# Long convolution and SiLU block on one core: token tiles of the second part 512 columns wide

## Chip, cores and metric

The kernel runs on 1 core of one Trainium2 chip. The metric is device time in microseconds (us). Three runs of the kernel before took 1626.51, 1628.32 and 1631.16 us; the median, 1628.32 us, is the number to beat.

## What is computed

Two parts follow one another. The first is a gated long convolution over 2 batches of 12480 tokens with 128 channels, by a transform of length 2 x 12480; the second is a two-layer block with SiLU between its weights, of 128 x 2048 and 2048 x 128:

```python
h_filt = (np.maximum(pos_emb @ w1, 0.0) @ w2) * np.exp(-0.01 * pos)[:, None]
u = x * v
y = np.fft.irfft(np.fft.rfft(u, n=L, axis=1) * np.fft.rfft(h_filt, n=L, axis=0)[None], n=L, axis=1)[:, :S]
attn = (x * y).reshape(B * S, D)
h = attn @ w_in
out = (h / (1.0 + np.exp(-h))) @ w_out
```

All is fp32. The second part takes each product as three fp32r matmuls: a value a is kept as a high part (a rounded to fp32r) and a low part (a minus the high part), and high x high, low x high and high x low are summed in PSUM.

## The kernel before

**The transform.** 12480 tokens are padded to 2 halves (i = 0, 1) of R = 98 rows by C = 64 columns. A first stage works along R (`stage_a`, L217, matmuls into tile ap), then for each of 49 pairs of frequencies a second stage goes forward (`pair_u`, tile up), multiplies by the filter and goes back (`pair_w`, tile wp; both at L419), and stores to DRAM (wd, L474). The last inverse stage is `attn_tile` (L611): for a token tile of up to five of the 64 columns it makes the blocks of 98 or 97 tokens in a PSUM bank yp, multiplies by x (L622, tile att) and splits the product into ah and al (L623, L624). Its inputs are fetched by `load_tile` (L594 from wd, L599 from x) into one buffer each.

**Token tiles.** `token_tiles` gives 52 tiles: for each batch and half twelve of five columns and one of four. Their widths are 490 (12 x), 392, 486 (12 x), 388, and the same again for the second batch, 24984 token columns in all.

**The second part** is one loop over steps (n, f), token tile n and one of NF = 16 slices f of the hidden dimension, 832 steps. A step issues three matmuls for the hidden slice (L813, L814, L815, into hq), ScalarE's SiLU (L820), the high part (L822 on VectorE, or L824 on ScalarE for some f), the low part (L825 on VectorE), and then, three steps late (`lag=3`), the three matmuls of an older slice into the output bank op (L841, L842, L843). After f = 15 the output is copied (L846) and stored. `attn_tile(n + 1)` is issued at f = 8 and `load_tile(n + 2)` at f = 9, so that ah and al of the next tile are ready before f = 0.

**What runs beside it.** The first batch's convolution is done before the loop starts, as are 7 of the 32 groups of the second batch's first stage. The rest of the second batch's convolution is a generator, `batch1_steps`, of 666 small side steps. The loop takes from it at each step in proportion, so that it has ended after `n_side` = 384 steps: two tiles before the last tile of the first batch has been used. All engines run in program order. PE gets its order from this loop, SP (the queue of loads) too: behind a load that waits for its buffer, all later loads wait. In the shared part the SiLU writes back into hq (three PSUM banks); after it, into a tile g in SBUF.

```python
steps = [(n, f) for n in range(len(tiles)) for f in range(NF)]
if f == 8 and n + 1 < len(tiles):
    attn[n + 1] = attn_tile(n + 1, *ahead.pop(n + 1), pmy, ("yp", 1))
if f == 9 and n + 2 < len(tiles):
    ahead[n + 2] = load_tile(n + 2)
while done < total and done * n_side < (s + 1) * total:
    done += next(side, total)
```

Of the kernel before, what the change touches and what calls it, by code (L numbers as in the profile page):

```python
# [10 lines left out]
F32 = mybir.dt.float32  # L11
F32R = mybir.dt.float32r
U32 = mybir.dt.uint32
AF = mybir.ActivationFunctionType
ALU = mybir.AluOpType
# [17 lines left out]
NF = DFF // 128  # L33
# [15 lines left out]
def tile_widths(i, n):  # L49

    if i == 0:
        return [98] * n
    w = [97] * n
    if n % 2:
        w[-1] = 98
    return w


def tile_offsets():
    offs, o = [], 0  # L60
    for b, i, t2, n in token_tiles():
        offs.append(o)
        o += sum(tile_widths(i, n))
    return offs, o


P = dict(
# [22 lines left out]
def kernel(  # L90
# [16 lines left out]
    nc = tc.nc  # L107
    ctx.enter_context(tc.manual_schedule())

    def pool(name, **kw):  # L110
        kw.setdefault("bufs", 1)
        return tc.alloc_tile_pool(name=name, reuse_waits="tile", **kw)
# [116 lines left out]
    def slot(o, n=512):  # L229

        return slots.rearrange("p k n -> p (k n)")[:, o : o + n]
# [128 lines left out]
    for t in P["seq"]:  # L360
# [9 lines left out]
        elif t == "p":  # L370
            g = len(pts)
            pts.append(wprep.tile([128, NP, R], F32, name=f"pt{g}", tag="pt", bufs=P["pb"]))
            for o in range(0, NP, 4) if g == 0 else [0]:
                n = 4 if g == 0 else NP
# [154 lines left out]
    pp = pool("pp2", space=PSUM)  # L529
# [6 lines left out]
    for it in range(-1, NQ):  # L536
# [7 lines left out]
        if 0 <= q < NQ:  # L544
            up = pair_u(0, q, pp, [(fbs[q][:, :, 0], X[:, 2 * q : 2 * q + 2])], nb)
            _, uw = times_i(0, q, rp, up, nb)
# [19 lines left out]
        if 0 <= q < NQ:  # L566
            hab = habs.pop(q)
            _, at = pair_p(0, q, rp, up, hab, 0, "at", nb, nc.vector)
            _, bt = pair_p(0, q, rp, uw, hab, 1, "bt", nb, nc.gpsimd)
# [15 lines left out]
    php.release()  # L585
    psa = pool("psa3", space=PSUM)
    tiles = token_tiles()
    offs, _ = tile_offsets()

    def load_tile(n):  # L590
        b, i, t2, m = tiles[n]
        w = sum(tile_widths(i, m))
        wt = slot(4096, 2 * 5 * D)[0:R].rearrange("p (c n) -> p c n", c=2)
        nc.sync.dma_start(  # L594
            out=wt[:, :, 0 : m * D],
            in_=wd[b][:, i].rearrange("k (c t) d -> k c (t d)", c=2)[:, :, t2 * D : (t2 + m) * D],
        )
        xs = slot(4096 + 2 * 5 * D, 490)
        nc.sync.dma_start(out=xs[:, 0:w], in_=xt[:, offs[n] : offs[n] + w])  # L599
        return wt, xs  # L600

    def attn_tile(n, wt, xs, psp, tag):
        b, i, t2, m = tiles[n]
        ws = tile_widths(i, m)
        w = sum(ws)
        yp = psp.tile([128, 512], F32, name=f"yp{n}", tag=tag[0], bufs=tag[1])
        o = 0
        for t in range(m):
            for c in range(2):
                for h in range(0, D, 64):  # L610
                    nc.tensor.matmul(  # L611
                        yp[h : h + 64, o : o + ws[t]],
                        wt[:, c, t * D + h : t * D + h + 64],
                        fai_sb[:, c, 0 : ws[t]],
                        start=(c == 0),
                        stop=(c == 1),
                    )
            o += ws[t]
        at = mt.tile([128, 490], F32, name=f"att{n}", tag="att", bufs=1)
        ah = mt.tile([128, 512], F32R, name=f"ah{n}", tag="ah", bufs=2)  # L620
        al = mt.tile([128, 512], F32R, name=f"al{n}", tag="al", bufs=2)
        nc.vector.tensor_tensor(out=at[:, 0:w], in0=yp[:, 0:w], in1=xs[:, 0:w], op=ALU.mult)  # L622
        nc.scalar.copy(out=ah[:, 0:w], in_=at[:, 0:w])  # L623
        nc.vector.tensor_tensor(out=al[:, 0:w], in0=at[:, 0:w], in1=ah[:, 0:w].bitcast(F32), op=ALU.subtract)  # L624
        return ah, al

    ahead, attn = {}, {}
    n_a = n_t = n_h = n_l = 0
    n_r = 4
    for t in P["seq3"]:  # L630
        if t == "x":
            uv.load()
        elif t in "md":
            uv.mul(nc.vector if t == "d" else nc.gpsimd)
        elif t in "Aa":
            stage_a_group(1, n_a, psa, uss.pop(n_a), 2, t == "A")
            n_a += 1
        elif t == "s":
            pair_s(*prods[NQ - 1])
        elif t == "v":  # L640
            pair_v(prods[NQ - 1][0], nc.vector)
        elif t == "u":
            last_w(NQ - 2)
        elif t == "U":
            last_w(NQ - 1)
            rp.release()
            rpa.release()
            mw = pool("mw")
            wo_split[:] = (mw.tile([128, NF * D], F32R, name=f"wo{k}") for k in "hl")
            mt = pool("mt")  # L650
        elif t == "S":
            nc.scalar.activation(out=warm_sb, in_=w2_sb[0:1, 0:1], func=AF.Silu)
        elif t == "L":
            ahead[n_t] = load_tile(n_t)
            n_t += 1
        elif t == "r":
            load_raw(n_r, spare[:, (n_r - 4) // 2 * 2, 256 * (n_r % 2) : 256 * (n_r % 2) + 256], wod)
            n_r += 1
        elif t == "h":
            split_hi(n_h, wo_split)  # L660
            n_h += 1
        elif t == "l":
            split_lo(n_l, wo_split)
            n_l += 1
        elif t == "Y":
            attn[0] = attn_tile(0, *ahead.pop(0), pp, ("up", 2))
    NA = n_a
    woh, wol = wo_split
    wih, wil = wi_split
# [5 lines left out]
    moe = pool("moe")  # L675
    fr = pool("fr")
    pmy = pool("pmy", space=PSUM)
# [4 lines left out]
    class Carved:  # L682


        at = dict(hab=(0,), at=(1024,), bt=(1792,), uw=(2560,), ws=(3072,), fb=(3584, 5868))
# [108 lines left out]

    pools = [psa]
    side = batch1_steps()
    n_side = (len([t for t in tiles if t[0] == 0]) - 2) * NF
    total = 2 * P['ya'] * (D // 4 - NA) + P['pd'] * NQ + max(P['off'].values()) - min(P['off'].values()) + 1
    done = 0
    steps = [(n, f) for n in range(len(tiles)) for f in range(NF)]  # L800
    LAG = P['lag']
    if P.get("cut2"):
        steps = steps[:P['cut2']]
    gs = {}
    op = {}
    for s in range(len(steps) + LAG):
        if s < len(steps):
            n, f = steps[s]
            w = sum(tile_widths(*tiles[n][1::2]))
            ah, al = attn[n]  # L810
            hp = pm.tile([128, 512], F32, name=f"hq{s}", tag="hq", bufs=3)
            fs = slice(f * 128, (f + 1) * 128)
            nc.tensor.matmul(hp[:, 0:w], wih[:, fs], ah[:, 0:w], start=True, stop=False)  # L813
            nc.tensor.matmul(hp[:, 0:w], wih[:, fs], al[:, 0:w], start=False, stop=False)  # L814
            nc.tensor.matmul(hp[:, 0:w], wil[:, fs], ah[:, 0:w], start=False, stop=True)  # L815
            beside = done < total
            g = hp if beside else moe.tile([128, 490], F32, name=f"g{s}", tag="g", bufs=2)
            gh = moe.tile([128, 512], F32R, name=f"gh{s}", tag="gh", bufs=P['lag'] + 1)
            gl = moe.tile([128, 512], F32R, name=f"gl{s}", tag="gl", bufs=P['lag'] + 1)
            nc.scalar.activation(out=g[:, 0:w], in_=hp[:, 0:w], func=AF.Silu)  # L820
            if f % P['fp'] if beside else f % P['fg']:
                nc.vector.tensor_copy(gh[:, 0:w], g[:, 0:w])  # L822
            else:
                nc.scalar.copy(out=gh[:, 0:w], in_=g[:, 0:w])  # L824
            nc.vector.tensor_tensor(out=gl[:, 0:w], in0=g[:, 0:w], in1=gh[:, 0:w].bitcast(F32), op=ALU.subtract)  # L825
            gs[s] = gh, gl
            if f == 8 and n + 1 < len(tiles):
                attn[n + 1] = attn_tile(n + 1, *ahead.pop(n + 1), pmy, ("yp", 1))
            if f == 9 and n + 2 < len(tiles):
                ahead[n + 2] = load_tile(n + 2)  # L830
            while done < total and done * n_side < (s + 1) * total:
                done += next(side, total)
        if s >= LAG:
            n, f = steps[s - LAG]
            w = sum(tile_widths(*tiles[n][1::2]))
            if f == 0:
                op[n] = pm.tile([128, 512], F32, name=f"op{n}", tag="op", bufs=2)
            o = op[n]
            fs = slice(f * 128, (f + 1) * 128)
            gh, gl = gs.pop(s - LAG)  # L840
            nc.tensor.matmul(o[:, 0:w], woh[:, fs], gh[:, 0:w], start=(f == 0), stop=False)  # L841
            nc.tensor.matmul(o[:, 0:w], woh[:, fs], gl[:, 0:w], start=False, stop=False)  # L842
            nc.tensor.matmul(o[:, 0:w], wol[:, fs], gh[:, 0:w], start=False, stop=(f == NF - 1))  # L843
            if f == NF - 1:
                ot = moe.tile([128, 490], F32, name=f"ot{n}", tag="ot", bufs=2)
                nc.scalar.copy(out=ot[:, 0:w], in_=o[:, 0:w])  # L846
                nc.scalar.dma_start(out=out[:, offs[n] : offs[n] + w], in_=ot[:, 0:w])
                del op[n], attn[n]
    if not P.get("cut2"):
        for _ in side:  # L850
# [85 lines left out]
```

## Time and profile before

| what | value |
|---|---|
| median of the runs | 1628.32 us |
| profiled execution, span from first to last instruction | 1624.7 us |
| PE busy | 1591.1 us, 98% of the span |
| VectorE (DVE) busy | 1285.6 us, 79% |
| ScalarE (ACT) busy | 1108.2 us, 68% |
| GpSimd (POOL) busy | 575.4 us, 35% |

The page gives the span of the profiled execution; no other time of that execution is recorded. It lies 3.6 us below the median of the runs. The second part's loop begins at about 329 us, the side steps end at about 988 us, and from there to the end only the second part and `attn_tile` run. PE's matmuls are pipelined: a matmul's recorded duration covers filling and draining, so the time that one more matmul costs is read from the distance between two starts.

### The profile page before, as it was taken

How to read it: one execution, taken by the hardware profiler on the slowest of the kernel's cores; microseconds unless marked ns; L12 is line 12 of the kernel's file. 1: busy time of each engine (PE TensorE's matmuls, PEld its weight loads, DVE VectorE, ACT ScalarE, POOL GpSimd, SP SyncE). 2: the span in 40 equal slices, each digit the busy share in tenths (PEclk: the TensorE clock that was granted, in tenths of full speed). 3: DMA queues.
4: the chain of work that ended last, by engine and by line, in shares of the span. 5: the costliest groups of instructions: out<-in, count | busy, mean ns of one | idle time of the engine just before them, and what ended most of it. 6: DMA issues, size and time to landing. Idle time of an engine off the chain costs nothing.

```text
span 1624.7 us, 27176 instructions
## 1 busy us (share of the span) xinstructions
PE 1591.1 (98%) x9376; PEld 1369.7 (84%) x9376; DVE 1285.6 (79%) x2182; ACT 1108.2 (68%) x2151; POOL 575.4 (35%) x564
## 2 busy tenths in 40 slices
PE   7899999899999999999999999999999999999999
PEld 6787777688888888988888888888888898888888
DVE  5979899765688889888888887777777777777776
ACT  5598898767777777777777775555555555555555
POOL 5627778632156656666666650000000000000000
PEclk9899999889999999999999999999999999999999
DMA  9838999854255554555554541111111111111110
GB/s 264 235 100 229 237 262 259 236 137 121 77 132 138 132 145 128 153 134 148 135 137 133 135 109 53 43 50 49 33 47 48 47 43 38 44 50 47 35 41 18
DMA packets 130001, 186.99 MB, mean 115 GB/s; under 512 B 11346, under 2 KB 79608, under 8 KB 129864
## 3 DMA queue, kind: packets, MB, share of 16 engines
q1 hardware_dynamic: 89480, 147.58, 33.2%
q10 hardware_dynamic: 40384, 37.67, 8.3%
q8 instruction: 75, 1.23, 0.3%
q14 instruction: 62, 0.51, 0.1%
HBM read 125.36 MB, written 53.42 MB: 110 GB/s over the span
## 4 chain that ended last, share of the span: by engine, by line
PE 79%; DMA 1%; issue 0%; SPq 0%; POOL 0%; ACT 0%; DVE 0%; POOLq 0%
PE op L841 12%; PE op L843 11%; PE op L842 11%; PE hq L814 11%; PE hq L813 11%; PE hq L815 11%; PE yp L611 6%; PE wp L419 2%; PE up L419 2%; PE ap L217 2%; DMA slots<-in_v_dram 1%; DMA slots<-wd 0%; POOL slots L245 0%; SPq L240 0%; DVE att L622 0%
## 5 line engine op out<-in xcount | busy, mean ns | idle before, releaser
L820 ACT ACTIVATE g<-hq 128x486 f32<-128x486 f32 (+3 forms) x448 | 255.6, 570 | 224.2 <-PE hq L815 214.3
L825 DVE TENSOR_TENSOR gl<-g,gh 128x486 fp32r<-128x486 f32 (+3 forms) x448 | 294.4, 657 | 94.7 <-PE hq L815 59.4
L841 PE MATMUL op<-gh,woh 128*128 128x490 f32 (+3 forms) x832 | 323.4, 389 | 0.0
L814 PE MATMUL hq<-al,wih 128*128 128x490 f32 (+3 forms) x832 | 315.9, 380 | 0.0
L813 PE MATMUL hq<-ah,wih 128*128 128x490 f32 (+3 forms) x832 | 315.8, 380 | 0.0
L843 PE MATMUL op<-gh,wol 128*128 128x490 f32 (+3 forms) x832 | 315.4, 379 | 0.0
L815 PE MATMUL hq<-ah,wil 128*128 128x490 f32 (+3 forms) x832 | 315.4, 379 | 0.0
L842 PE MATMUL op<-gl,woh 128*128 128x490 f32 (+3 forms) x832 | 315.1, 379 | 0.0
L820 ACT ACTIVATE hq<-hq 128x490 f32<-128x490 f32 (+2 forms) x384 | 214.1, 559 | 93.8 <-PE hq L815 65.6
L825 DVE TENSOR_TENSOR gl<-hq,gh 128x490 fp32r<-128x490 f32 (+2 forms) x384 | 251.7, 662 | 32.6 <-ACT gh L824 22.1
L822 DVE CAST gh<-hq 128x490 fp32r<-128x490 f32 (+2 forms) x288 | 188.9, 656 | 50.0 <-ACT hq L820 48.4
L822 DVE CAST gh<-g 128x486 fp32r<-128x486 f32 (+3 forms) x336 | 137.7, 410 | 56.9 <-ACT g L820 54.9
L813 PEld LDWEIGHTS hq<-ah,wih 128*128 128x128 f32 x832 | 156.7, 188 | 25.6 <-DVE gl L825 0.8
L814 PEld LDWEIGHTS hq<-al,wih 128*128 128x128 f32 x832 | 156.6, 188 | 24.9
L841 PEld LDWEIGHTS op<-gh,woh 128*128 128x128 f32 x832 | 156.5, 188 | 24.9
L815 PEld LDWEIGHTS hq<-ah,wil 128*128 128x128 f32 x832 | 156.7, 188 | 24.6
L843 PEld LDWEIGHTS op<-gh,wol 128*128 128x128 f32 x832 | 156.3, 188 | 25.0
L842 PEld LDWEIGHTS op<-gl,woh 128*128 128x128 f32 x832 | 156.6, 188 | 19.7 <-DVE gl L825 0.3
L223 ACT COPY X<-ap 64x392 f32<-64x392 f32 x208 | 99.8, 480 | 34.4 <-PE ap L217 32.2
L611 PEld LDWEIGHTS yp<-fai_sb,slots 98*64 98x64 f32 x2048 | 89.3, 138 | 17.9 <-issue 16.7
L611 PE MATMUL yp<-fai_sb,slots 98*64 98x98 f32 (+1 forms) x2048 | 99.4, 252 | 0.3 <-DMA slots<-wd 0.3
L623 ACT CAST ah<-att 128x490 fp32r<-128x490 f32 (+3 forms) x52 | 30.9, 594 | 90.5 <-DVE att L622 90.5
(1068 smaller groups left out, 2546.7 us busy)
## 6 DMA issues: line engine op xcount, KB each, us to landing
slots<-hs SPq DMA_DIRECT2D x98, 256.0 KB
slots<-wd SPq DMA_DIRECT2D x48, 490.0 KB
hs<-hab SPq DMA_DIRECT2D x49, 256.0 KB
wd<-ws SPq DMA_DIRECT2D x49, 256.0 KB
slots<-in_fb_dram SPq DMA_DIRECT2D x49, 256.0 KB
wd<-slots ACTq DMA_DIRECT2D x49, 256.0 KB
fb<-in_fb_dram ACTq DMA_DIRECT2D x45, 256.0 KB
xs<-in_x_dram SPq DMA_DIRECT2D x32, 196.0 KB
```

Source lines behind the costliest of these rows:

```text
L223: nc.scalar.copy(out=o, in_=src[:, k0:k1])
L419: nc.tensor.matmul(out[:, k].rearrange("p i d -> p (i d)"), f[:, k], a[:, k], start=(i == 0), stop=(i == len(passes) - 1),)
L611: nc.tensor.matmul(yp[h : h + 64, o : o + ws[t]], wt[:, c, t * D + h : t * D + h + 64], fai_sb[:, c, 0 : ws[t]], start=(c == 0), stop=(c = ...
L813: nc.tensor.matmul(hp[:, 0:w], wih[:, fs], ah[:, 0:w], start=True, stop=False)
L814: nc.tensor.matmul(hp[:, 0:w], wih[:, fs], al[:, 0:w], start=False, stop=False)
L815: nc.tensor.matmul(hp[:, 0:w], wil[:, fs], ah[:, 0:w], start=False, stop=True)
L820: nc.scalar.activation(out=g[:, 0:w], in_=hp[:, 0:w], func=AF.Silu)
L822: nc.vector.tensor_copy(gh[:, 0:w], g[:, 0:w])
L825: nc.vector.tensor_tensor(out=gl[:, 0:w], in0=g[:, 0:w], in1=gh[:, 0:w].bitcast(F32), op=ALU.subtract)
L841: nc.tensor.matmul(o[:, 0:w], woh[:, fs], gh[:, 0:w], start=(f == 0), stop=False)
L842: nc.tensor.matmul(o[:, 0:w], woh[:, fs], gl[:, 0:w], start=False, stop=False)
L843: nc.tensor.matmul(o[:, 0:w], wol[:, fs], gh[:, 0:w], start=False, stop=(f == NF - 1))
```

## The change

The second part no longer walks over the 52 token tiles. `moe_tiles` cuts the 24984 token columns into 49 spans: a first one of 408 and 48 of 512. The inverse transform keeps its 52 tiles, but `attn_tile` now only writes its product into `ring`, an SBUF tile of 1024 columns that is used as a ring (in two pieces where a tile crosses its end, 24 times). A new `split_tile` makes ah and al of one span from the ring. The table `events` says at which step (n, f) each tile is produced: at f = 8 when the next span needs one new tile, at f = 2 and f = 8 when it needs two (spans 3, 19 and 35). A tile's load is issued one step after the tile before it was produced. `n_side` becomes the step at which tile 25, the last of the first batch, is produced: 360. There are 49 x 16 = 784 steps.

```diff
+WM = 512
+def moe_tiles():
+    total = tile_offsets()[1]
+    edges = [0, *range(total % WM or WM, total + 1, WM)]
+    return list(zip(edges, edges[1:]))
...
-        at = mt.tile([128, 490], F32, name=f"att{n}", tag="att", bufs=1)
-        nc.vector.tensor_tensor(out=at[:, 0:w], in0=yp[:, 0:w], in1=xs[:, 0:w], op=ALU.mult)
...
+        a = 0
+        while a < w:
+            p = (offs[n] + a + lead) % (2 * WM)
+            k = min(w - a, 2 * WM - p)
+            nc.vector.tensor_tensor(out=ring[0][:, p : p + k], in0=yp[:, a : a + k], in1=xs[:, a : a + k], op=ALU.mult)
+            a += k
+
+    def split_tile(n):
+        lo, hi = spans[n]
+        w = hi - lo
+        p = (lo + lead) % (2 * WM)
+        at = ring[0][:, p : p + w]
+        ah = mt.tile([128, WM], F32R, name=f"ah{n}", tag="ah", bufs=2)
+        al = mt.tile([128, WM], F32R, name=f"al{n}", tag="al", bufs=2)
+        nc.scalar.copy(out=ah[:, 0:w], in_=at)
+        nc.vector.tensor_tensor(out=al[:, 0:w], in0=at, in1=ah[:, 0:w].bitcast(F32), op=ALU.subtract)
         return ah, al
...
-    n_side = (len([t for t in tiles if t[0] == 0]) - 2) * NF
+    n_yp = 1
+    events = {}
+    first_b1 = next(k for k, t in enumerate(tiles) if t[0] == 1)
+    for n in range(len(spans)):
+        need = []
+        while n + 1 < len(spans) and n_yp < len(tiles) and offs[n_yp] < spans[n + 1][1]:
+            need.append(n_yp)
+            n_yp += 1
+        for k, f in zip(need, [8] if len(need) == 1 else [2, 8]):
+            events[n, f] = k
+    n_side = next(n * NF + f for (n, f), k in events.items() if k == first_b1 - 1)
...
-    steps = [(n, f) for n in range(len(tiles)) for f in range(NF)]
+    steps = [(n, f) for n in range(len(spans)) for f in range(NF)]
...
-            if f == 8 and n + 1 < len(tiles):
-                attn[n + 1] = attn_tile(n + 1, *ahead.pop(n + 1), pmy, ("yp", 1))
-            if f == 9 and n + 2 < len(tiles):
-                ahead[n + 2] = load_tile(n + 2)
+            if (n, f) in events:
+                attn_tile(events[n, f], *ahead.pop(events[n, f]), pmy, ("yp", 1))
+            if f == 8 and n + 1 < len(spans):
+                attn[n + 1] = split_tile(n + 1)
+            if (n, f - 1) in events and events[n, f - 1] + 1 < len(tiles):
+                ahead[events[n, f - 1] + 1] = load_tile(events[n, f - 1] + 1)
```

Tiles g and ot grow from 490 to 512 columns, and the output is stored by spans. In the changed file the loop's matmuls stand at L848 to L850 and L878 to L880, the SiLU at L855, the high and low parts at L857, L859 and L860, the inverse transform at L623, the product at L635 and the split at L645 and L646.

Two places show how the order moves. First PE, in the last stretch, around a tile of the inverse transform (yp): before, the steps around it are 490 columns wide.

```order
L813 MATMUL hq_13801<-ah_13592,wih 128x490
L814 MATMUL hq_13801<-al_13593,wih 128x490
L815 MATMUL hq_13801<-ah_13592,wil 128x490
L611 MATMUL yp_13811<-fai_sb,slots 64x98 x20
L841 MATMUL op_13745<-gh_13767,woh 128x490
L842 MATMUL op_13745<-gl_13768,woh 128x490
L843 MATMUL op_13745<-gh_13767,wol 128x490
```

In the changed kernel, at span 35, the same place reads as follows, first the tile of f = 2, and six steps later that of f = 8:

```order
L848 MATMUL hq_13774<-ah_13648,wih 128x512
L849 MATMUL hq_13774<-al_13649,wih 128x512
L850 MATMUL hq_13774<-ah_13648,wil 128x512
L623 MATMUL yp_13784<-fai_sb,slots 64x98 x16
L878 MATMUL op_13559<-gh_13740,woh 128x512
...
L850 MATMUL hq_13876<-ah_13648,wil 128x512
L623 MATMUL yp_13886<-fai_sb,slots 64x97 x16
L623 MATMUL yp_13886<-fai_sb,slots 64x98 x4
L878 MATMUL op_13820<-gh_13842,woh 128x512
```

Each step keeps its six matmuls, each of them wider, and 36 of them now lie between two tiles where there were 96.

Second VectorE at the same place. Before, the product (att) and the low part of the tile (al) follow one another:

```order
L825 TENSOR_TENSOR gl_13807<-g_13805,gh_13806 128x490
L622 TENSOR_TENSOR att_13832<-yp_13811,slots 128x490
L624 TENSOR_TENSOR al_13834<-att_13832,ah_13833 128x490
L822 CAST gh_13846<-g_13845 128x490
L825 TENSOR_TENSOR gl_13847<-g_13845,gh_13846 128x490
```

After, the first of two products stands alone between two steps, and only the second is followed by the split of 512 columns:

```order
L860 TENSOR_TENSOR gl_13780<-g_13778,gh_13779 128x512
L635 TENSOR_TENSOR ring<-yp_13784,slots 128x392
L857 CAST gh_13813<-g_13812 128x512
...
L860 TENSOR_TENSOR gl_13882<-g_13880,gh_13881 128x512
L635 TENSOR_TENSOR ring<-yp_13886,slots 128x486
L646 TENSOR_TENSOR al_13909<-ring,ah_13908 128x512
L857 CAST gh_13920<-g_13919 128x512
```

The split has come off the tile and stands once for each span.

## Rows read from the trace of the kernel before

**Rows 1.** The page: busy us (share of the span) xinstructions.
```profile
PE 1591.1 (98%) x9376; PEld 1369.7 (84%) x9376; DVE 1285.6 (79%) x2182; ACT 1108.2 (68%) x2151; POOL 575.4 (35%) x564
```

**Rows 2.** The page: chain of waits that ended last, shares by engine.
```profile
PE 79%; DMA 1%; issue 0%; SPq 0%; POOL 0%; ACT 0%; DVE 0%; POOLq 0%
```

**Rows 3.** Windows of the shared part and of the rest: us, engines' busy time, clock.
```profile
core 0: us, PE busy (x) PEld busy (x) DVE busy (x) ACT busy (x) POOL busy (x), PEclk, DMA share, GB/s
329.20:988.00 658.80, 658.03 (x4050) 576.48 (x4049) 550.99 (x875) 499.03 (x973) 361.88 (x367) 1.00 0.48 129
988.00:1624.70 636.70, 633.17 (x3742) 544.30 (x3740) 461.74 (x838) 351.95 (x614) 0.00 (x0) 1.00 0.15 42
```

**Rows 4.** Timeline of PE, 490 columns: start us, us, engine line op out<-in.
```profile
1239.77 0.38 PE L813 MATMUL hq<-ah,wih 128*128 128x490 f32 x1
...
1243.73 0.38 PE L813 MATMUL hq<-ah,wih 128*128 128x490 f32 x1
```

**Rows 5.** Timeline of PE, 486 columns.
```profile
1402.14 0.38 PE L841 MATMUL op<-gh,woh 128*128 128x486 f32 x1
...
1404.56 0.38 PE L815 MATMUL hq<-ah,wil 128*128 128x486 f32 x1
```

**Rows 6.** Timeline of PE, 392 columns.
```profile
1309.67 0.34 PE L813 MATMUL hq<-ah,wih 128*128 128x392 f32 x1
...
1313.40 0.34 PE L841 MATMUL op<-gh,woh 128*128 128x392 f32 x1
```

**Rows 7.** Timeline of PE, 388 columns.
```profile
1609.79 0.34 PE L815 MATMUL hq<-ah,wil 128*128 128x388 f32 x1
...
1613.39 0.34 PE L842 MATMUL op<-gl,woh 128*128 128x388 f32 x1
```

**Rows 8.** Timeline of PE, 256 columns, six fp32r matmuls of a side step.
```profile
592.01 0.28 PE L419 MATMUL up<-xs13h,fw13h 128*128 128x256 f32 x1
...
592.72 0.39 PE L841 MATMUL op<-gh,woh 128*128 128x490 f32 x1
```

**Rows 9.** Groups by shape: the same VectorE and ScalarE work at two widths.
```profile
L825 DVE TENSOR_TENSOR gl<-g,gh 128x490 fp32r<-128x490 f32 x192 | 128.7, 671 | 41.9 <-PE hq L815 28.7 <-ACT gh L824 8.2
L820 ACT ACTIVATE g<-hq 128x490 f32<-128x490 f32 x192 | 111.6, 581 | 97.7 <-PE hq L815 94.2 <-DVE gh L822 0.5
L825 DVE TENSOR_TENSOR gl<-g,gh 128x388 fp32r<-128x388 f32 x32 | 18.0, 563 | 4.8 <-ACT gh L824 4.0
L820 ACT ACTIVATE g<-hq 128x388 f32<-128x388 f32 x32 | 15.8, 494 | 13.0 <-PE hq L815 11.6 <-DVE gl L825 1.0
```

**Rows 10.** Timeline of PE and SP around a tile: yp, then the next load.
```profile
1084.96 1.91 PE L611 MATMUL yp<-fai_sb,slots 98*64 98x98 f32 x40
...
1086.92 0.34 SPq L594 DMA_DIRECT2D slots<-wd  x1
```

**Rows 11.** Windows around that load; the last two columns are DMA share and GB/s.
```profile
1088.90:1091.40 2.50, 2.50 (x13) 2.14 (x12) 1.46 (x4) 1.68 (x4) 0.00 (x0) 1.00 0.79 251
1091.40:1093.40 2.00, 2.00 (x11) 1.71 (x10) 1.77 (x4) 0.83 (x2) 0.00 (x0) 1.00 0.00 0
```

**Rows 12.** Timeline of VectorE and PE at a step where PE was late for hq.
```profile
482.13 0.67 DVE L825 TENSOR_TENSOR gl<-hq,gh 128x490 fp32r<-128x490 f32 x1
...
482.61 0.38 PE L843 MATMUL op<-gh,wol 128*128 128x490 f32 x1
482.86 0.49 PE L813 MATMUL hq<-ah,wih 128*128 128x490 f32 x1
```

**Rows 13.** Timeline of the end: last matmul, output copy and store.
```profile
1620.83 0.34 PE L843 MATMUL op<-gh,wol 128*128 128x388 f32 x1
1621.21 0.48 ACT L846 COPY ot<-op 128x388 f32<-128x388 f32 x1 [1.31 <-PE op L843]
1621.72 0.34 ACTq L847 DMA_DIRECT2D out_dram<-ot  x1
```

More of the change, by code (lines that the diff above doesn't have):

```diff
@@ L587 @@
     tiles = token_tiles()
-    offs, _ = tile_offsets()
+    offs, n_tokens = tile_offsets()
+    spans = moe_tiles()
+    lead = -spans[0][1] % WM
     def load_tile(n):
@@ L618, in attn_tile @@
             o += ws[t]
-        at = mt.tile([128, 490], F32, name=f"att{n}", tag="att", bufs=1)
-        ah = mt.tile([128, 512], F32R, name=f"ah{n}", tag="ah", bufs=2)
-        al = mt.tile([128, 512], F32R, name=f"al{n}", tag="al", bufs=2)
-        nc.vector.tensor_tensor(out=at[:, 0:w], in0=yp[:, 0:w], in1=xs[:, 0:w], op=ALU.mult)
-        nc.scalar.copy(out=ah[:, 0:w], in_=at[:, 0:w])
-        nc.vector.tensor_tensor(out=al[:, 0:w], in0=at[:, 0:w], in1=ah[:, 0:w].bitcast(F32), op=ALU.subtract)
+        a = 0
[13 more added lines that the diff above has]
+        nc.vector.tensor_tensor(out=al[:, 0:w], in0=at, in1=ah[:, 0:w].bitcast(F32), op=ALU.subtract)
         return ah, al
-    ahead, attn = {}, {}
+    ahead, attn, ring = {}, {}, []
     n_a = n_t = n_h = n_l = 0
@@ L650 @@
             mt = pool("mt")
+            ring.append(mt.tile([128, 2 * WM], F32, name="ring"))
         elif t == "S":
@@ L665 @@
         elif t == "Y":
-            attn[0] = attn_tile(0, *ahead.pop(0), pp, ("up", 2))
+            attn_tile(0, *ahead.pop(0), pp, ("up", 2))
+            attn[0] = split_tile(0)
     NA = n_a
@@ L796 @@
     side = batch1_steps()
-    n_side = (len([t for t in tiles if t[0] == 0]) - 2) * NF
+    n_yp = 1
[8 more added lines that the diff above has]
+            events[n, f] = k
+    assert n_yp == len(tiles)
+    n_side = next(n * NF + f for (n, f), k in events.items() if k == first_b1 - 1)
     total = 2 * P['ya'] * (D // 4 - NA) + P['pd'] * NQ + max(P['off'].values()) - min(P['off'].values()) + 1
     done = 0
-    steps = [(n, f) for n in range(len(tiles)) for f in range(NF)]
+    steps = [(n, f) for n in range(len(spans)) for f in range(NF)]
     LAG = P['lag']
@@ L808 @@
             n, f = steps[s]
-            w = sum(tile_widths(*tiles[n][1::2]))
+            w = spans[n][1] - spans[n][0]
             ah, al = attn[n]
@@ L816 @@
             beside = done < total
-            g = hp if beside else moe.tile([128, 490], F32, name=f"g{s}", tag="g", bufs=2)
+            g = hp if beside else moe.tile([128, 512], F32, name=f"g{s}", tag="g", bufs=2)
             gh = moe.tile([128, 512], F32R, name=f"gh{s}", tag="gh", bufs=P['lag'] + 1)
@@ L834 @@
             n, f = steps[s - LAG]
-            w = sum(tile_widths(*tiles[n][1::2]))
+            w = spans[n][1] - spans[n][0]
             if f == 0:
@@ L844 @@
             if f == NF - 1:
-                ot = moe.tile([128, 490], F32, name=f"ot{n}", tag="ot", bufs=2)
+                ot = moe.tile([128, 512], F32, name=f"ot{n}", tag="ot", bufs=2)
                 nc.scalar.copy(out=ot[:, 0:w], in_=o[:, 0:w])
-                nc.scalar.dma_start(out=out[:, offs[n] : offs[n] + w], in_=ot[:, 0:w])
+                nc.scalar.dma_start(out=out[:, spans[n][0] : spans[n][1]], in_=ot[:, 0:w])
                 del op[n], attn[n]
```

## The prediction, on record before the changed kernel ran

> **What bounds the kernel now.** I read the page's busy shares first: PE is busy for 1591.1 of 1624.7 us, the next engine (VectorE) for 79% [rows 1]. The chain of waits says the same: PE holds 79% of it and no other engine more than 1% [rows 2]. Busy time of pipelined matmuls can mislead, so the windows come next: in the part shared with the second batch's convolution (329 to 988 us) PE has 658.0 of 658.8 us, in the rest 633.2 of 636.7, at granted clock 1.00, the 2.4 GHz level; VectorE has 551.0 and 461.7, ScalarE 499.0 and 352.0 [rows 3]. So from 329 us on the time is the sum of PE's matmuls, and what a change is worth is what it takes from that sum. The timelines of PE then give the price of one matmul, as the distance between starts where nothing else stands between.
>
> **The price by width.** 490 columns: 18 matmuls in 1243.73 - 1239.77 = 3.96 us, 0.2200 each [rows 4]. 486 columns: 11 in 2.42 us, also 0.2200 [rows 5]. 392 columns: 21 in 3.73 us, 0.1776 [rows 6]. 388 columns: 20 in 3.60 us, 0.1800 [rows 7]; I take 0.1788 for these two. 256 columns: 6 in 0.71 us, 0.1183 [rows 8]. The reader is to see that four columns fewer are worth nothing, twice: 486 costs what 490 costs, 388 no less than 392. Per column at 2.4 GHz, four would be 1.7 ns. So the price goes up in steps of columns. Blocks of 16 fit: 486 and 490 both end in the 31st block, 388 and 392 in the 25th, 256 at the end of the 16th; a block then costs (220.0 - 178.8)/6 = 6.9 ns and (178.8 - 118.3)/9 = 6.7 ns, and 16 columns at 2.4 GHz are 6.7 ns. Blocks of 8 do not fit (486 would be one below 490). A tile of 490 columns pays for 496.
>
> **Part 1: wider steps.** The kernel before has 768 steps of 486 or 490 columns and 64 of 388 or 392, six matmuls each: 768 x 6 x 0.2200 = 1013.8 and 64 x 6 x 0.1788 = 68.7, together 1082.5 us. The changed one has 768 steps of 512 columns and 16 of 408. No row shows 512. Bounds: from the 490 row one block more, 220.0 + 6.9 = 226.9 ns; from the 256 row, the other full multiple of 16, 16 blocks more at 6.67, 118.3 + 106.7 = 225.0. I take 226.0, nearer the 490 row. From below, were the blocks 32 wide, 512 would cost what 490 does, 220.0; from above, were the price a straight line through 256 and 488 columns (0.438 ns a column), 230.6. 408 columns are the 26th block, 178.8 + 6.7 = 185.5. New sum: 768 x 6 x 0.2260 = 1041.4, and 16 x 6 x 0.1855 = 17.8, together 1059.2 us. **Gain: 23.3 us** (27.9 at 225.0, 19.1 at 226.9).
>
> The row at 490 columns shows 220.0 ns, that is 15.8 ns over 490 / 2.4. The Trainium skill (TensorE: Matmul & The Clock Gate, "Back-to-back issue gap") gives N / 2.4 + 2.5 ns at the full clock, with no steps. By it 490 columns would be 206.7 ns, which the trace contradicts, and the change, with the same columns in 288 fewer matmuls, would save 0.7 us.
>
> **Part 2: the inverse transform.** It keeps its 52 tiles and all their matmuls, 1.85 us each from yp to the next step's first matmul [rows 10]; its interruptions stay 52. Cost on the path: 0.
>
> **Part 3: ring and split.** From 388 to 490 columns the low part goes from 563 to 671 ns, the SiLU from 494 to 581 [rows 9]: 1.06 and 0.85 ns a column, some 0.15 us an instruction that does not depend on width. VectorE gets 24 instructions more for tiles that cross the ring's end and loses about 85 with the 48 steps; ScalarE loses some 60. Both get lighter by about 10 us. Their cover is PE, with 27% of VectorE's time free in the last stretch [rows 3], so I book 0. The split is used seven steps after f = 8, about 9.5 us later, and needs three instructions of 0.7 us.
>
> **Part 4: two tiles in one span**, three times. The second tile's load waits for the first tile's yp, then is needed six steps later. Before, SP issues it 1086.92 - 1084.96 = 1.96 us after yp began [rows 10], and DMA is silent after 1091.4 [rows 11]: landed within 6.4 us of yp's start. The new distance is 1.85 + 36 x 0.226 = 10.0 us, and more in spans 3 and 19, where side work stands between. Margin 3.6 us, so 0; without it each us of lateness costs PE one us, three times, at most some 10 us if the load took twice as long.
>
> **Part 5: the side steps end earlier**, 666 in 360 steps for 384. The matmuls of the second part take 368 x 6 x 0.220 + 16 x 6 x 0.1788 = 502.9 of the shared 658.8 us, the rest is 155.9. After: 344 x 6 x 0.226 + 17.8 + 155.9 = 640.2 us. Side steps come 2.9% denser. VectorE had 551.0 of 658.8 us, 84%; it loses some 15 us there (fewer steps, 1.7% fewer columns), 536 of 640, again 84%. PE was late for a bank of hq in two places of the shared part; at one of them the low part ended at 482.80 and PE began at 482.86, 0.25 after its previous start instead of 0.22, and the next start lost 0.1 [rows 12]. I book 0.5 us for a few more such places.
>
> **Part 6: the end.** The last span has 512 columns, the last tile had 388. After the last hidden slice come SiLU, high part, low part, the last matmuls, the copy and the store [rows 13]; 124 columns more cost 3 x 0.11 on ScalarE, 0.13 on VectorE, 0.1 on PE: 0.6 us.
>
> **Sum:** -23.3 + 0.5 + 0.6 = -22.2 us. On the profiled execution 1624.7 becomes 1602.5 us; the median of the runs lies 3.6 us above its span, so 1628.3 becomes **1606 us**.
>
> **Rivals.**
>
> *Straight line.* Each matmul pays its columns and a constant, and 486 at 0.2200 is chance. 512 columns then cost 229.6 (from the 490 row, 22 x 0.438) to 230.6 ns, and 408 some 186: 1058.0 to 1062.6 plus 17.9, a gain of 2 to 6.6 us, less the 1.1 of parts 5 and 6: 1623 to 1627.5 us. For it: 256, 390 and 488 columns lie near one line. Against: the two equal pairs, and a slope of 0.438 where the clock gives 0.417.
>
> *Wider blocks.* With blocks of 32, 512 costs 220.0: 1013.8 + 17.8 = 1031.6, a gain of 50.9, 1578.5 us. For it: both pairs are equal here too. Against: the blocks would cost 41.2/3 = 13.7 and 60.5/5 = 12.1 ns, further apart than with 16, around 13.3.
>
> *VectorE becomes the bound of the shared part (slower).* The margin in [rows 12] is nothing in two steps, and the side steps come denser per step, 1.85 for 1.73. If the low part came late at every step, PE would wait at every third bank of hq. To undo the gain each of the 360 steps must lose over 22.2 / 360 = 62 ns; at the 0.14 us lost in [rows 12] it would be 50 us, 1656 us. Against: 84% before and after, and only two places in 384 steps.
>
> *The change does not do what it says.* In the new order the loop's matmuls are 512 wide, so this has no chance of its own.
>
> **Chances.** Forecast (blocks of 16): 0.76. Straight line 0.14, wider blocks 0.05, VectorE 0.05. The forecast's own range is 1601.5 (225.0 ns) to 1610.5 us (226.9 ns), with 4 below for a price between the blocks and 10 above for part 4. The range for 8 in 10 takes in the forecast and the faster part of the straight line: **1597 to 1624 us**; outside lie wider blocks, the slower rival and most of the line. A measurement of this kernel can tell about 0.3%, 4.9 us, from no change. Faster by more (below 1623.4): 0.76 + 0.05 + a little of the line, 0.83; within: 0.12; slower: 0.05.
>
> **What would show it.** In the new profile the starts of 512-column matmuls lie 0.226 us apart (0.220: wider blocks, 0.230: the line); the tail from the last side matmul on has no waits on PE; yp at span 35, f = 8, starts without waiting for a DMA; VectorE's share of the shared part stays near 84%, and PE's starts for hq there show no gaps but a few of 0.1 us. The prediction is wrong if a distance other than 0.225 to 0.227 stands there, or if PE waits for hq in most steps of the shared part.

## Result and the profile after

The changed kernel takes 1614.84 us (median of 4 runs, 1613.84 to 1617.68) beside 1629.65 us of the kernel before: ratio 0.9912, 95% interval 0.9896 to 0.9928. A second set of runs gave 1615.84 beside 1629.80, ratio 0.9904 (0.9877 to 0.9931). The forecast was 1606 us: right in direction and inside its range, the gain about two thirds of the one worked out.

The page's busy shares answer to [rows 1]:

```profile
PE 1575.6 (98%) x9088; PEld 1318.0 (82%) x9088; DVE 1273.1 (79%) x2119; ACT 1098.6 (68%) x2085; POOL 575.6 (36%) x564
```

The windows from the loop's first matmul on, the shared part and then the part after it, answer to [rows 3] and have its columns:

```profile
336.40:978.00 641.60, 640.88 (x3891) 546.01 (x3891) 539.75 (x839) 488.56 (x936) 360.96 (x366) 1.00 0.48 133
978.00:1615.90 637.90, 634.24 (x3612) 522.48 (x3611) 463.21 (x811) 352.51 (x584) 0.00 (x0) 1.00 0.14 42
```

PE is as full as before, VectorE's share of the shared part is still 84%. The loop has 1279.5 us where it had 1295.5, 16.0 less. The loop's matmuls hold all of it: summing, for each of them, the distance to PE's next start gives 1098.2 us before and 1082.2 after. In these two executions the loop starts at other times. Its first matmul on PE's timeline of the kernel before:

```profile
329.26 0.87 PE L813 MATMUL hq<-ah,wih 128*128 128x490 f32 x1
```

And of the changed kernel:

```profile
336.49 0.80 PE L848 MATMUL hq<-ah,wih 128*128 128x408 f32 x1
```

The code ahead of it is the same but for the first tile's product and split. In the profiled executions of this study the loop began between 329.3 and 339.8 us, so the span of one execution (1615.9 after) tells less than the loop. The price of 512 columns, on PE's timeline, answers to [rows 4]:

```profile
1245.79 0.39 PE L878 MATMUL op<-gh,woh 128*128 128x512 f32 x1
...
1248.51 0.39 PE L878 MATMUL op<-gh,woh 128*128 128x512 f32 x1
```

Twelve matmuls in 2.72 us are 0.2267 us each, one block of 16 columns over 0.2200. The yp pair of span 35 starts 9.88 us apart with no wait before the second, as worked out:

```profile
1280.60 1.57 PE L623 MATMUL yp<-fai_sb,slots 98*64 98x98 f32 x32
...
1290.48 1.90 PE L623 MATMUL yp<-fai_sb,slots 98*64 98x97 f32 x40
```

### The profile page after: what moved, and what is told of

It is laid out like the page before. It is cut to its first block, busy times and chain, and to the rows that moved or that the text cites. A ratio compares the mean times of both kernels' runs of the same rounds, so it can differ in the third digit from the quotient of the medians.

```text
span 1615.9 us, 26412 instructions
## 1 busy us (share of the span) xinstructions
PE 1575.6 (98%) x9088; PEld 1318.0 (82%) x9088; DVE 1273.1 (79%) x2119; ACT 1098.6 (68%) x2085; POOL 575.6 (36%) x564
## 4 chain that ended last, share of the span: by engine, by line
PE 79%; DMA 1%; ACT 0%; DVE 0%; issue 0%; POOL 0%; POOLq 0%; SPq 0%
PE op L878 12%; PE op L879 11%; PE hq L848 11%; PE op L880 11%; PE hq L850 11%; PE hq L849 11%; PE yp L623 6%; PE ap L227 2%; PE wp L429 2%; PE up L429 2%; DMA slots<-wd 1%; DMA wd<-ws 0%; ACT X L233 0%; DVE X L235 0%; DVE wol L500 0%
## 5 line engine op out<-in xcount | busy, mean ns | idle before, releaser
L855 ACT ACTIVATE g<-hq 128x512 f32<-128x512 f32 x424 | 254.0, 599 | 227.5 <-PE hq L850 220.3
L860 DVE TENSOR_TENSOR gl<-g,gh 128x512 fp32r<-128x512 f32 x424 | 293.7, 693 | 95.0 <-PE hq L850 67.2
L878 PE MATMUL op<-gh,woh 128*128 128x512 f32 (+1 forms) x784 | 313.2, 399 | 0.0
L848 PE MATMUL hq<-ah,wih 128*128 128x512 f32 (+1 forms) x784 | 306.2, 391 | 0.3 <-DVE gl L860 0.3
L879 PE MATMUL op<-gl,woh 128*128 128x512 f32 (+1 forms) x784 | 305.6, 390 | 0.0
L849 PE MATMUL hq<-al,wih 128*128 128x512 f32 (+1 forms) x784 | 305.2, 389 | 0.0
L850 PE MATMUL hq<-ah,wil 128*128 128x512 f32 (+1 forms) x784 | 305.0, 389 | 0.0
L880 PE MATMUL op<-gh,wol 128*128 128x512 f32 (+1 forms) x784 | 304.6, 389 | 0.0
L855 ACT ACTIVATE hq<-hq 128x512 f32<-128x512 f32 (+1 forms) x360 | 206.9, 578 | 91.4 <-PE hq L850 71.4
L860 DVE TENSOR_TENSOR gl<-hq,gh 128x512 fp32r<-128x512 f32 (+1 forms) x360 | 244.8, 685 | 30.4 <-ACT gh L859 20.6
L857 DVE CAST gh<-hq 128x512 fp32r<-128x512 f32 (+1 forms) x270 | 183.6, 680 | 52.2 <-ACT hq L855 50.6
L857 DVE CAST gh<-g 128x512 fp32r<-128x512 f32 x318 | 135.7, 427 | 60.7 <-ACT g L855 60.3
L848 PEld LDWEIGHTS hq<-ah,wih 128*128 128x128 f32 x784 | 147.4, 188 | 32.1 <-DVE gl L860 1.2
L850 PEld LDWEIGHTS hq<-ah,wil 128*128 128x128 f32 x784 | 147.5, 188 | 30.8
L880 PEld LDWEIGHTS op<-gh,wol 128*128 128x128 f32 x784 | 147.2, 188 | 30.6
L878 PEld LDWEIGHTS op<-gh,woh 128*128 128x128 f32 x784 | 147.5, 188 | 29.6
L879 PEld LDWEIGHTS op<-gl,woh 128*128 128x128 f32 x784 | 147.7, 188 | 24.6 <-DVE gl L860 0.3
L623 PEld LDWEIGHTS yp<-fai_sb,slots 98*64 98x64 f32 x2048 | 89.3, 138 | 21.7 <-issue 17.9
L623 PE MATMUL yp<-fai_sb,slots 98*64 98x98 f32 (+1 forms) x2048 | 99.4, 252 | 3.5 <-DMA slots<-wd 3.5
```

What stands on the lines that cost most here:

```text
L623: nc.tensor.matmul(yp[h : h + 64, o : o + ws[t]], wt[:, c, t * D + h : t * D + h + 64], fai_sb[:, c, 0 : ws[t]], start=(c == 0), stop=(c = ...
```

## Experiments

**1. Is the price a staircase?** In a kernel that is otherwise the changed one, the second part works on fewer columns, span by span, and leaves the rest of their output out:

```diff
+    stair = [512, 510, 504, 500, 498, 496, 494, 490, 488, 484, 482, 480, 478, 472, 466, 464, 462, 448, 432, 418, 416, 400, 384, 512]
+    used[24:48] = stair
-            w = spans[n][1] - spans[n][0]
+            w = used[n]
```

> The 512-column kernel, but in spans 24 to 46 the second part works on the first 512, 510, 504, 500, 498, 496, 494, 490, 488, 484, 482, 480, 478, 472, 466, 464, 462, 448, 432, 418, 416, 400 and 384 columns only; the rest of those spans' output is left out. Blocks of 16: the distance of two starts is 0.2267 us for 512 down to 498, 0.2200 for 496 to 482, 0.2133 for 480 to 466, 0.2067 for 464 and 462, 0.200 for 448, 0.193 for 432 and 418, 0.187 for 416, 0.180 for 400, 0.173 for 384. Straight line: it falls by 0.3 to 0.44 ns with each column and shows no flats.

PE's timeline of this kernel, each pair of rows 30 matmuls apart (five steps):

```profile
1031.22 0.39 PE L851 MATMUL hq<-ah,wih 128*128 128x512 f32 x1
1038.02 0.39 PE L851 MATMUL hq<-ah,wih 128*128 128x512 f32 x1
...
1126.51 0.39 PE L851 MATMUL hq<-ah,wih 128*128 128x498 f32 x1
1133.31 0.39 PE L851 MATMUL hq<-ah,wih 128*128 128x498 f32 x1
...
1150.14 0.39 PE L851 MATMUL hq<-ah,wih 128*128 128x496 f32 x1
1156.85 0.39 PE L851 MATMUL hq<-ah,wih 128*128 128x496 f32 x1
...
1266.65 0.38 PE L851 MATMUL hq<-ah,wih 128*128 128x482 f32 x1
1273.25 0.38 PE L851 MATMUL hq<-ah,wih 128*128 128x482 f32 x1
...
1314.05 0.37 PE L851 MATMUL hq<-ah,wih 128*128 128x478 f32 x1
1320.45 0.37 PE L851 MATMUL hq<-ah,wih 128*128 128x478 f32 x1
...
1359.05 0.38 PE L851 MATMUL hq<-ah,wih 128*128 128x466 f32 x1
1365.44 0.38 PE L851 MATMUL hq<-ah,wih 128*128 128x466 f32 x1
```

512 and 498 columns both take 6.80 us for 30, 0.2267 each; 482 takes 0.2200, 478 and 466 both 0.2133. Over the same distance 510, 504 and 500 gave 0.2267, 490 and 488 0.2200, 472 0.2133. Flats of 16 columns, 6.7 ns apart: the straight line falls. Three things are not as written down. Widths at the upper end of a flat pay half a step more than those below them on it: 496 is at 0.2236 (494 too), 480 at 0.2167; 464, with 0.2100, also lies between two flats. And 484 at 0.2187 and 462 at 0.2118 lie off theirs; below them 448, 432 and 416 columns stand 1 to 3 ns above what was expected, 418 columns, at 0.190, 3 ns below, and only 400 and 384 on it. The third is that two widths have two prices. The flats above were read behind yp in each span; ahead of yp, with the same tiles, 500 columns cost 0.2233 and 488 cost 0.2257. For 488, 30 matmuls ahead of yp and 30 behind it:

```profile
1208.94 0.38 PE L851 MATMUL hq<-ah,wih 128*128 128x488 f32 x1
1215.71 0.39 PE L851 MATMUL hq<-ah,wih 128*128 128x488 f32 x1
...
1219.10 0.38 PE L851 MATMUL hq<-ah,wih 128*128 128x488 f32 x1
1225.70 0.38 PE L851 MATMUL hq<-ah,wih 128*128 128x488 f32 x1
```

The granted clock is 1.00 in both stretches and PE has no wait in either. So the width sets the price here within some 6 ns, and something that changes inside a span moves it.

**2. Two columns more or less, in whole kernels.** `WM = 498` and `WM = 496`, with ah, al and ring kept at their sizes:

> Spans of 498 columns instead of 512 (50 of 498 and a first one of 84). Blocks of 16: 498 columns are two more than 31 full blocks, so a matmul costs what 512 columns cost, 0.2267 us: 800 x 6 x 0.2267 + 96 x about 0.052 = 1093 us of loop matmuls where the kernel before has 1082.5; about 1640 us, 0.6% slower than before. Straight line between 490 (0.2200) and 512 (0.2270): 0.2225 us, 1073 us, about 1620 us. The distance of two starts tells them apart: 0.2267 or 0.2225.

> Spans of 496 columns (50 of 496 and a first one of 184). Blocks of 16: 31 full blocks, so the same 0.2200 us as 490 columns: 800 x 6 x 0.2200 + 96 x 0.092 = 1065 us, within 3 us of the 512-column kernel, about 1617 us, and some 25 us under the kernel with 498 columns, which differs by two columns. Straight line: 0.2219 us a matmul, and only 2 to 3 us between 496 and 498.

PE's timeline of the kernel with 498 columns, two rows 24 matmuls apart:

```profile
1299.70 0.39 PE L848 MATMUL hq<-ah,wih 128*128 128x498 f32 x1
...
1305.14 0.39 PE L848 MATMUL hq<-ah,wih 128*128 128x498 f32 x1
```

And of the one with 496, two rows 18 matmuls apart:

```profile
1300.00 0.39 PE L848 MATMUL hq<-ah,wih 128*128 128x496 f32 x1
...
1304.02 0.39 PE L848 MATMUL hq<-ah,wih 128*128 128x496 f32 x1
```

24 matmuls in 5.44 us are 0.2267 at 498 columns; 18 in 4.02 us are 0.2233 at 496. The medians are 1667.8 us (ratio 1.0216, 1.0183 to 1.0249) and 1637.3 (1.0044, 1.0015 to 1.0074): both kernels are 20 to 28 us over what was expected. The price of 498 columns is the expected one; for 496 it is half a step higher (4800 x 3.4 ns = 16 us), so two columns cost 17.5 us by the distances (1100.3 and 1082.8 us over the 4799 wide matmuls), where 25 were expected and 2 to 3 by the straight line. Most of what the kernel with 498 columns is over, and with it most of the rest of the 30 us between the medians, goes with the clock. It was granted at 0.50, the 1.2 GHz level, from 328 us until 379.2 us with 498 columns and from 331.5 until 369.0 with 496; in the changed kernel it rose at 338.7, 2.2 us into the loop. With 498 columns PE was busy for 13.5 of the 17 us before it fell and for 44.35 of the 45.30 us of the loop before it rose. That stretch, and one at full clock with 496 columns (columns as in [rows 3]):

```profile
333.90:379.20 45.30, 44.35 (x195) 43.41 (x194) 11.78 (x39) 19.65 (x52) 10.73 (x10) 0.50 0.36 107
...
372.40:374.00 1.60, 1.60 (x17) 1.60 (x16) 0.00 (x0) 1.56 (x4) 0.84 (x1) 1.00 0.24 72
```

PE's rows in them, two 9 matmuls apart at 84 columns, two 14 apart at 184:

```profile
370.22 0.42 PE L880 MATMUL op<-gh,wol 128*128 128x84 f32 x1
372.14 0.42 PE L850 MATMUL hq<-ah,wil 128*128 128x84 f32 x1
...
372.42 0.27 PE L848 MATMUL hq<-ah,wih 128*128 128x184 f32 x1
373.98 0.27 PE L850 MATMUL hq<-ah,wil 128*128 128x184 f32 x1
```

A narrow matmul costs 0.2133 us at the lower level, with 84 and with 184 columns, and 0.111 at the full one (84 columns 0.11 as well, after 380 us), where 0.05 and 0.09 were expected. An estimate for 498 columns: about half of PE's 44.35 us, some 22 us, is the clock, and 96 x 0.06 = 6 us the dearer narrow matmuls, together the 28. The ten runs with 496 columns go from 1631 to 1650 us, the slowest at granted clocks of 0.981 to 0.985, the four below 1634.3 at 0.989 to 0.992; those four fit 1617 + 16, and the profiled one is the slowest. Why the clock rose late here was not tested.

**3. The change without its width.** `WM = 490`, ring, split and events as in the change:

> Ring, split and events as in the changed kernel, but spans of 490 columns (50 of 490 and a first one of 484), so 816 steps where the kernel before has 832. If the gain is the price of 512 columns, a matmul stays at 0.2200 us and only the 16 steps go: 816 x 6 x 0.2200 = 1077 us for 1082.5, about 5 us under the kernel before and 10 us over the changed one. If the gain came from the ring and the split, it would be there at 490 columns too: some 15 us under the kernel before.

1623.64 us beside 1629.80, ratio 0.9964 (0.9947 to 0.9981); the loop's matmuls sum to 1092.9 us (before 1098.2, changed 1082.2), 490 columns at 0.2200. The 16 steps less that 490-column spans allow bring 5 us; the ring and the split cost and bring nothing more; the rest of the gain hangs on 512.

**4. The same kernel 32 bytes further on in SBUF.**

```diff
     const = pool("const")
+    const.tile([128, 8], F32, name="pad")
```

> The 512-column kernel with one unused tile of 32 bytes a partition ahead of all others, so that the columns that stream (ah, al, gh, gl) and the second weights start on a multiple of 64 bytes instead of 32 past one. If the blocks are pieces of 64 bytes in SBUF, a row of 2048 bytes touches 32 of them instead of 33 and each matmul gets one block (6.7 ns) cheaper: 0.2200 us, 31 us less in all, about 1585 us. If the blocks are counted from the first column, nothing changes: 0.2267 us and about 1615 us.

PE's timeline of the shifted kernel:

```profile
1299.84 0.40 PE L849 MATMUL hq<-ah,wih 128*128 128x512 f32 x1
1300.08 0.39 PE L850 MATMUL hq<-al,wih 128*128 128x512 f32 x1
1300.31 0.39 PE L851 MATMUL hq<-ah,wil 128*128 128x512 f32 x1
1300.54 0.39 PE L879 MATMUL op<-gh,woh 128*128 128x512 f32 x1
1300.76 0.39 PE L880 MATMUL op<-gl,woh 128*128 128x512 f32 x1
1300.99 0.40 PE L881 MATMUL op<-gh,wol 128*128 128x512 f32 x1
1301.22 0.39 PE L849 MATMUL hq<-ah,wih 128*128 128x512 f32 x1
```

Neither outcome that was written down: the price rose. A step takes 1.38 us, 0.231 a matmul, and unevenly (0.227 after L879 and L880, up to 0.235 after L881). The loop's matmuls sum to 1100.4 us, and the median is 1631.94 beside 1632.23, ratio 1.0002 (0.9985 to 1.0020). An unused tile of 32 bytes takes away the whole gain.

**5. Which places are good?** The first idea, columns and weights at the same place modulo 64 bytes, was put to two kernels: all weights shifted as well (`mwi.tile([128, 8], F32, name="rpad")` behind wih and wil), and the weights shifted by 16 bytes (tiles 16 elements longer, `[:, 4 : 4 + DFF]`; the columns move by 128 bytes with them). The changed kernel ran beside them once more.

> As the run with the unused 32 bytes ahead of all tiles, but the first weights (wih, wil) are shifted by 32 bytes too, so that all weights and all streamed columns start on a multiple of 64 bytes. If what counts is that the columns and the weights loaded beside them start at the same place modulo 64 bytes, all six matmuls of a step are back at 0.2270 us and the loop at 1279 us, about 1615 us. If a stream that starts on a multiple of 64 bytes is dearer in itself, they cost 0.233 us or more, and the loop takes 1298 us or more.

> The changed kernel with all weights starting 16 bytes further on, the streamed columns where they were. If weights and columns must start at the same place modulo 64 bytes, each of the six matmuls costs more than 0.2270 us: 0.2285 us if a quarter of 64 bytes costs a quarter of the 6.7 ns, 0.234 us if any offset costs all of it. If a multiple of 16 bytes is enough, 0.2270 us.

> The changed kernel once more, on the chip of the next three. Every theory: 512 columns at 0.2270 us, the loop from its first matmul to the end near 1279 us, some 15 us under the kernel before.

All on multiples of 64 bytes: 1629.93 us, ratio 1.0003 (0.9989 to 1.0017), 1098.7 us of loop matmuls. Weights 16 bytes on: 1631.16 us in one run, 1097.8. The changed kernel repeated: 1082.2. So the idea falls: at the same place modulo 64 bytes the price stayed at 0.231. The next kernels moved the streamed columns span by span, with tiles of WM + 32 columns from which a slice is taken, the weights at 96 (first) or 0 (second) modulo 128 bytes:

```diff
-        ah = mt.tile([128, WM], F32R, name=f"ah{n}", tag="ah", bufs=2)
+        ah = mt.tile([128, WM + 32], F32R, name=f"ah{n}", tag="ah", bufs=2)[:, oa[n] : oa[n] + WM]
```

> The changed kernel, with the streamed columns (ah, al, gh, gl) of spans 24 to 41 starting 0, 4, 8, 12, 16, 24, 32 ... 120 bytes further on, span by span, and the weights where they are; spans 42 to 47 shift ah, al and gh, gl differently. What counts is read from each span's distance of starts. If streamed columns and weights must start at the same place modulo 128 bytes, only the span at 0 bytes has 0.2270 us and the others 0.229 to 0.234. If modulo 64, the span at 64 bytes has it too. If only multiples of 64 bytes are bad, 32 bytes and its neighbours are dear and the rest cheap. If the place does not matter and the padding did something else, all are at 0.2270.

> The same shifts, with every weight and every unshifted stream starting on a multiple of 128 bytes. If what counts is the distance between streamed columns and weights, each span costs what it costs in the run with the weights at 96 bytes. If what counts is each one's own place, the spans move by 32 bytes: what stands there at 0 bytes stands here at 96.

All spans of the last part of both lie between 0.231 and 0.238 us (means over a span, dearest at 4 bytes), those at 0 bytes too, whose columns and weights stand as in the changed kernel modulo 128 bytes; only the distance between the tiles had grown, from 2048 to 2176 bytes. Single runs: 1640.96 and 1640.33 us; loop matmuls 1101.8 and 1104.0. No rule on the place modulo 128 bytes explains the 0.2267 us.

**6. Does the kernel before hang on its place too?** The pad of experiment 4, in the kernel before:

> The kernel before, with its tiles of 490 and 486 columns, and the same unused 32 bytes a partition ahead of all tiles that took the whole gain from the changed kernel. If 512 columns were cheap in the changed kernel because the width is cheap, and the padding spoils any width, 490 columns too rise from 0.2200 us, by some 4 ns as 512 did: 4608 x 0.0045 = 21 us, about 1650 us, and the gain of the width is still there between the two padded kernels. If the changed kernel only met a lucky place in SBUF, and 490 columns had an ordinary one, 0.2200 us stays and so do about 1630 us: then at an ordinary place the two widths take the same time.

PE's timeline of the kernel before with the pad, two rows 24 matmuls apart:

```profile
1239.52 0.38 PE L814 MATMUL hq<-ah,wih 128*128 128x490 f32 x1
...
1244.80 0.38 PE L814 MATMUL hq<-ah,wih 128*128 128x490 f32 x1
```

24 matmuls in 5.28 us, 0.2200: 490 columns hardly mind the shift (0.2205 on average over the last part, 0.2201 without the pad). 1631.56 us, ratio 1.0008 (0.9995 to 1.0020). At five other placements 512 columns cost 0.231 to 0.233 on average there, and the change then takes as long as the kernel before or longer; at the one that the change happens to have they cost 0.227.

**7. The covers that were booked at nothing.** Tiles of a double span at f = 6 and 8 (`[8] if len(need) == 1 else [6, 8]`), and `n_side = 240`:

> Two things at once, read at different places. First, the two tiles of spans 3, 19 and 35 come at f = 6 and f = 8 instead of f = 2 and f = 8, so the second tile's yp follows the first after 1.85 + 12 x 0.227 = 4.6 us where the load lands some 5.4 to 6.4 us after it: PE waits 1 to 2 us before the second yp at span 35, 3 to 5 us in all. If the load is no cover at all (lands in time anyway), no wait. Second, the 666 side steps end after 240 steps instead of 360, 2.8 for each step. If VectorE and GpSimd have room, PE's matmuls for hq in the shared part keep their distances and the total changes by no more than the first effect, near 1620 us. If the shared part was near its bound, the steps are held up by tenths of a us each: 25 us or more, 1640 us or more.

PE's timeline at span 35 (what a row waited for stands at its end, in us):

```profile
1357.22 1.57 PE L623 MATMUL yp<-fai_sb,slots 98*64 98x98 f32 x32
...
1363.40 1.90 PE L623 MATMUL yp<-fai_sb,slots 98*64 98x97 f32 x40 [1.67 <-DMA slots<-wd]
```

The window of 500 to 780 us, in the shared part (columns as in [rows 3]):

```profile
500.00:780.00 280.00, 256.97 (x1486) 207.82 (x1484) 231.86 (x346) 211.24 (x408) 230.19 (x230) 0.99 0.57 153
```

At span 35 the second yp waits 1.67 us for its load and begins 6.18 us after the first: the load's cover was real, its margin 9.88 - 6.18 = 3.7 us. The whole takes 1690.59 us in the one run. With 2.8 side steps for each step GpSimd is busy for 82% of the window (66% in the changed kernel), VectorE for 83% (90%), and the loop is 75 us longer (1355.1 for 1280.0). PE, which waits 1 us in the changed kernel's loop, waits 49 us: 25 of them are side matmuls (L429) released by GpSimd's low parts, 6 the loads of the three double spans; the rest goes to other releasers, 10 of it to none that the profile shows. So the shared part has a bound, below 2.8 side steps a step and above the 1.85 of the change.

## Why the prediction was right, and where it was off

- **What bounds** the kernel: right. All of the loop's 16.0 us came out of the distances between starts of its matmuls.
- **Price in blocks of 16**: right in the main; experiments 1 and 2 show flats of 16 columns at most widths from 466 to 512, and the rivals *straight line* and *wider blocks* fall. Not foreseen: 480 and 496 columns, at the upper end of a flat, cost half a block more, and 488 and 500 have two prices in one span. The formula that the prediction sets beside its price is given by the Trainium skill (TensorE: Matmul & The Clock Gate, "Back-to-back issue gap") for an isolated matmul, and the section says that it over-counts a stream of long ones; by it 512 columns would be 215.8 ns, and the runs here show 226.7, more and not less.
- **The step that was off is part 1's price of 512 columns**, a term of the sum that was mis-sized: taken as 226.0 ns between 225.0 and 226.9, it is 226.7, 4608 x 0.7 ns = 3 us of the 6 that are missing. The other 3.5 us lie in the shared part: by all distances there between two of the loop's matmuls, the 512-column ones cost 230.7 ns and the first span's 88 distances 218 (185.5 was taken), 10.5 us over the flats, where the kernel before had 7.0; part 5 booked 0.5 us. (By its own terms the upper end of the forecast's own range is 1610.3, not 1610.5 us; nothing hangs on it.)
- **A reason that was missing**: the price of 512 columns was taken as a matter of width alone. Experiments 4 to 6 show that it rises, by 4 to 6 ns, when the tiles are shifted in SBUF, and 4 ns are the whole gain; 490 columns hardly showed this. That the measured time lies near the forecast is thus luck of the place: the kernels of experiments 4 and 5 that ran ten times, equal in width and order, took 1631.94 and 1629.93 us, outside the range. Which property of the place decides stays open: the place modulo 64 or 128 bytes does not, and nothing was run to tell the tiles' distance from the side on which other engines read. Nor is it shown that the place acts by itself: the two prices of 488 columns stand on the same tiles, so the timing beside the other engines remains a rival. Whether 504 columns, in the middle of a flat, would keep 0.2267 at any place was not tried.
- **Parts 2 to 4**: right; yp still takes 1.84 us from the path, experiment 3 shows the ring and split at nothing, experiment 7 the load's margin (3.6 us worked out, 3.7 measured).
- **Part 5 and the slower rival**: VectorE stayed at 84% and did not decide. Where the shared part does become the bound, about half of PE's waiting is for GpSimd's work for the side matmuls, and next to none is for hq.
- **From the span to the runs**: the loop gained 16.0 us, the medians 14.8 and 14.0. Every run on record for which both are listed takes 1.7 to 2.1 us more than its span, so the 3.6 us that the prediction adds are in part the scatter of the runs. What lies ahead of the loop differs from execution to execution; whether the change adds 1 to 2 us there isn't settled.

## What to carry to other kernels

Where PE is full, read the price of a matmul as the distance of starts at every width that the trace has, and look for equal prices at unequal widths: here, at 466 to 512 columns, time goes up in steps of 16 with some exceptions, so a width just past a step pays for columns that it doesn't use. Before a gain of a per cent is put down to a size, run the same kernel with its buffers shifted by some bytes, and the kernel before as well. A narrow rest span need not be cheap: a matmul of 84 columns cost here what one of 184 did, and in those executions the clock rose some 30 to 40 us later. Read the granted clock of a stretch before its price is put down to a width.

## What was not expected of the hardware

- 32 unused bytes ahead of the tiles changed the mean distance of 512-column fp32r matmuls from 0.227 to 0.231 us, 18 us in 4608, and left 490 columns at 0.2200 to 0.2205.
- fp32r matmuls of 84 and of 184 columns, each with its weight load, were both 0.213 us apart at the 1.2 GHz level and 0.11 at the 2.4 GHz level.
- Two full multiples of 16 columns (496 and 480) stood about 3.5 ns above the narrower widths of their own flat, while 512 at the changed kernel's place stood on the flat of 498 to 510.
